# Reordering the first loads and two groups of matmuls in a linear-attention block on one core

## The chip, the core and the metric

The kernel runs on one NeuronCore of a Trainium2 chip. The core has a matrix engine (PE, with its weight loads listed as PEld), a vector engine (DVE), an activation engine (ACT, also called ScalarE), a general engine (POOL, also called GpSimd) and a queue engine (SP, also called SyncE). The engines run their own instruction streams in order and wait for each other by semaphores. DMAs are issued by SP and by ACT here, and 16 DMA engines of the core carry them. The metric is the device time in microseconds (us); the smaller, the better.

## The reference

One transformer block in bfloat16 with 2048 positions and width 640. With LN a layer norm without learned scale:

```python
h   = x + A(LN(x))            # linear attention, 32 heads of 20
out = h + B(LN(h))            # GEGLU: (gelu(h @ w_gate) * (h @ w_up)) @ w_down, inner width 1536

# A:
q, k, v = split(LN(x) @ wqkv)                 # each 2048 x 640, by heads
pq, pk  = q @ w_phi, k @ w_phi                # per head, 20 x 20
phi(y)  = [softmax(y), softmax(-y)]           # 40 features per head
kv, z   = phi(pk).T @ v, sum(phi(pk))         # over all positions
o       = (phi(pq) @ kv) / (phi(pq) . z + 1e-6)
A       = o @ wo
```

## The kernel before, in words

The 2048 positions are 16 tiles of 128, four to a block of 512. Tile t of `x` is `x_sb[t // 4][:, t % 4, :]`. The text calls tiles 0 to 3 x0 to x3.

The program is one hand-written order of instructions (L186 to L860) with no planner; each engine runs its instructions in the order in which they are written.

**Front (L186 to L491).** SP issues the loads of x0, x1, x2, two chunks of `Wv` (row blocks 0-1 and 2-3 of the v part of wqkv, 320 KB each), x3, the last `Wv` chunk (row block 4, 160 KB), tiles 4 and 5 of x, and then five transposing loads of the k part (`load_T`, L202). ACT issues only `wphi` (25 KB, 640 rows of 40 bytes) and then loads its function table (L191). PE warms up on constants. For tiles 0 and 1, x minus its mean (`xc`, L271 and L423) is transposed by PE and copied to `LN1T` by ACT (L164); the scale 1/std is applied later, when v is evicted (`v_ev`, L315). Tile 1's mean comes from an ACT pass (`st_act`, L406), tiles 0, 2, 3 and on from `BN_STATS` on DVE (L120). `v_part(t, *cs)` issues the matmuls of v of tile t for row blocks cs (two each, L311). `ln_tp(2)` is PE's transpose of tile 2 (L163) and DVE's copy of it (L164), which stands on DVE between the two statistics of tile 3. `root[0]()` is the pair Ln, Exp on ACT (L130, L131) that gives 1/std of tile 3. `fold` (L231) multiplies w_phi into the k part of wqkv, 128 rows at a time, by PE (L247), evicted by ACT (L256) or DVE (L258).

**The k loop (L493 to L533).** For each tile: k features by PE, exp(k) and exp(-k) on ACT (L339), their sums and reciprocals on DVE (L346, L350), the division by POOL and DVE (L354), v of a later tile (L295), and, for groups of tiles, the accumulation of phi(k).T @ v in one PSUM tile `kvp` (`kv_tile`, L373). Towards its end come the first q products, four groups.

**Turn (L534 to L542 and L782 to L833).** After the last `kv_tile`, DVE copies and masks `kvp` and transposes it into `KV[0]` and `KV[1]`, one for each sign of phi (L380, L382). `q_mm(j, part, kcs)` is the product of q of group j: two parts of five matmuls of 512 columns (L395), and `q_exp` its two exponentials on ACT (L400). `attn_a(t)` is phi(q) @ KV of tile t: 20 small products on `KV[0]`, then 20 on `KV[1]` (L587), and the copies of the result to `AB` by ACT and DVE (L606).

**The rest (L849 to L859)** weaves the gate/up matmuls (L721), the down matmuls (L740) and the remaining attention steps of each tile.

PSUM has four two-bank buffers in this half of the program, which all of `tp`, `pv`, `wa`, `pk`, `pq`, `ab` share (`gtile`, L110): a tile waits for the eviction of the one whose buffer it takes.

Of the kernel before, what the change touches and what calls it, by code (L numbers as in the profile page):

```python
# [17 lines left out]
def kernel(  # L18
# [12 lines left out]
    nc = tc.nc  # L31
    P = 128
    S = 2048
    D = 640
# [5 lines left out]
    NC = D // P  # L40
# [31 lines left out]
    x_v = A_x.rearrange("b (p t) d -> p (b t) d", t=NT)  # L72
    o_v = out.rearrange("b (p t) d -> p (b t) d", t=NT)
    w_v = A_wqkv.rearrange("(c p) n -> p c n", p=P)
# [9 lines left out]
    x_sb = [const.tile([P, 4, D], BF16, name=f"x_sb{b}") for b in range(NB)]  # L84
# [25 lines left out]
    def gtile(name):  # L110
        return psG.tile([P, 2, 512], F32, name=name, tag="G")

    def ln_stats(pool, tiles, tag, act=True, between=None, log=False):

        n = len(tiles)
        mv = small(pool, [P, n, nc.vector.BN_AGGR_DIM], "mv" + tag)
        stats = small(pool, [P, n, 2, nc.vector.BN_STATS_DIM], "stats" + tag)
        for j, xt in enumerate(tiles):
            for i in range(2):
                nc.vector.bn_stats(stats[:, j, i, :], xt[:, i * HD:(i + 1) * HD])  # L120
                if between and i == j == 0:
                    between()
        for j in range(n):
            nc.vector.bn_aggr(mv[:, j, :], stats[:, j])
        ve = small(pool, [P, n], "ve" + tag)
        rstd = small(pool, [P, n], "rstd" + tag)
        if log is not False:

            def root():
                nc.scalar.activation(ve, mv[:, :, 1], ACTF.Ln, bias=eps)  # L130
                nc.scalar.activation(rstd, ve, ACTF.Exp, scale=-0.5)  # L131

            if log is True:
                root()
            else:
                log.append(root)
        else:
            nc.gpsimd.tensor_scalar_add(ve, mv[:, :, 1], EPS)
            nc.gpsimd.tensor_tensor(rstd, ve, nhalf[:, 0:n], op=ALU.pow)

        mr = small(pool, [P, n], "mr" + tag)
        if act:
            for j in range(n):
                nc.gpsimd.tensor_scalar(mr[:, j:j + 1], mv[:, j, 0:1], rstd[:, j:j + 1], -1.0,
                                        op0=ALU.mult, op1=ALU.mult)
        return [(xt, mv[:, j, 0:1], rstd[:, j:j + 1], mr[:, j:j + 1]) for j, xt in enumerate(tiles)]
# [11 lines left out]
    def transpose_to(dst, src, on_pe, on_dve=False):  # L158

        if on_pe:  # L160
            tp = psG.tile([P, 16, P], BF16, name="tp", tag="G")
            for c in range(NC):
                nc.tensor.transpose(tp[:, c, :], src[:, c * P:(c + 1) * P], ident)  # L163
            (nc.vector.tensor_copy if on_dve else nc.scalar.copy)(dst, tp[:, 0:NC, :])  # L164
        else:
            nc.sync.dma_start_transpose(dst, src)
# [8 lines left out]
    Wv = p1.tile([P, NC, D], BF16, name="Wv")  # L175
# [9 lines left out]

    nc.gpsimd.memset(nhalf, -0.5)  # L186
    nc.gpsimd.memset(eps, EPS)
    nc.sync.dma_start(x_sb[0][:, 0:1, :], x_v[:, 0:1, :])
    nc.sync.dma_start(x_sb[0][:, 1:2, :], x_v[:, 1:2, :])
    nc.scalar.dma_start(wphi, phi_v.rearrange("(c p) f -> p c f", p=P))  # L190
    nc.scalar.add_instruction(mybir.InstLoadActFuncSet(name=nc.get_next_instruction_name(), act_func_set_id=6))  # L191
    nc.sync.dma_start(x_sb[0][:, 2:3, :], x_v[:, 2:3, :])
    nc.sync.dma_start(Wv[:, 0:2, :], w_v[:, 0:2, 2 * D:3 * D])
    nc.sync.dma_start(Wv[:, 2:4, :], w_v[:, 2:4, 2 * D:3 * D])
    nc.sync.dma_start(x_sb[0][:, 3:4, :], x_v[:, 3:4, :])
    nc.sync.dma_start(Wv[:, 4:5, :], w_v[:, 4:5, 2 * D:3 * D])
    nc.sync.dma_start(x_sb[1][:, 0:2, :], x_v[:, 4:6, :])

    def load_T(WT, i, *ds):
# [74 lines left out]
    def ln_st(*tiles, act=True, between=None, log=False):  # L274
        for t, v in zip(tiles, ln_stats(p1, [x_sb[t // 4][:, t % 4, :] for t in tiles], "1", act, between, log)):
            lnp[t] = v
# [8 lines left out]
    def ln_tp(t, on_dve=False):  # L285
        transpose_to(LN1T[t // 4][:, :, t % 4 * P:(t % 4 + 1) * P], lnp[t], True, on_dve)

    def lnT(t, c):
        b, tl = divmod(t, 4)
        return LN1T[b][:, c, tl * P:(tl + 1) * P]  # L290
# [14 lines left out]
    def v_part(t, *cs):  # L305

        if 0 in cs:
            pv[t] = gtile("pv")
        for c in cs:
            for u in range(2):  # L310
                nc.tensor.matmul(pv[t][:, u, 0:HD], lhsT=lnT(t, c), rhs=Wv[:, c, u * HD:(u + 1) * HD],  # L311
                                 start=(c == 0), stop=(c == NC - 1))

    def v_ev(t):
        nc.scalar.activation(vS[t % NV][:, :, 1:VC].rearrange("p (u h) f -> p u h f", u=2),  # L315
                             pv[t][:, :, 0:HD].rearrange("p u (h f) -> p u h f", f=Dh), ACTF.Copy,
                             scale=lnp[t][2] if t in CT else 1.0)
# [68 lines left out]
    def q_mm(j, part=(0, 1), kcs=range(NC)):  # L386

        if 0 in part and 0 in kcs:
            pqs[j] = gtile("pq")
        for i, bc in enumerate(QG[j]):  # L390
            if i not in part:
                continue
            b, c = divmod(bc, NC)
            for kc in kcs:
                nc.tensor.matmul(pqs[j][:, i, :], lhsT=Wq2[:, kc, c * P:(c + 1) * P], rhs=LN1T[b][:, kc, :],  # L395
                                 start=(kc == 0), stop=(kc == NC - 1))

    def q_exp(j, signs=(0, 1)):
        for s in signs:
            nc.scalar.activation(Eq[j][:, :, s, :], pqs[j][:, 0:len(QG[j])], ACTF.Exp, scale=(1.0, -1.0)[s])  # L400
# [49 lines left out]
    v_part(0, 2, 3)  # L450
    root = []
    ln_st(3, act=False, between=lambda: ln_tp(2, True), log=root)
    v_part(1, 2, 3)
    v_part(0, 4)
    root[0]()
    v_ev(0)
    v_part(1, 4)
    v_ev(1)
    v_part(2, *range(NC))
# [74 lines left out]
    q = len(QT)  # L534
# [67 lines left out]
    def attn_a(t, dve=0):  # L602
        attn_a_mm(t)
        AB, ab = ABs[t % 2], st[t, "ab"]
        for u in ((1, 0) if t in (4,) else (0, 1)):
            (nc.vector.tensor_copy if u >= 2 - dve else nc.scalar.copy)(  # L606
                AB[:, :, u * UH:(u + 1) * UH].rearrange("p s (r h) f -> p r s (h f)", r=2),
                ab[u][:, :, 0:2 * QH * KC].rearrange("p r (s x) -> p r s x", s=2))
        st[t] = AB
# [170 lines left out]


    q_mm(q, (0,))  # L782
    q_mm(q, (1,), (0, 1))
    attn_a(0, 1)
    q_mm(q, (1,), (2, 3, 4))
    q_exp(q)
    q_mm(q + 1)
    attn_b(0, True)
# [102 lines left out]
```

## Time and profile before

| what | us |
|---|---|
| median of 3 runs (272.98 to 273.24) | 272.99 |
| the profiled execution | 272.91 |
| its span, first to last instruction | 271.1 |
| PE busy in the span | 265.3 |
| DVE busy | 175.1 |
| ACT busy | 137.9 |
| POOL busy | 100.7 |
| granted clock of PE | 0.999 |

The profile lists instructions with their start from the beginning of the span, their length, the engine, the line of the kernel, and what they write and read (out<-in). A bracket at the end says how long the engine stood idle before the instruction and what ended the idle time. PE's matmuls are pipelined: they overlap, so the length of one is more than the distance to the next. A line that stands for several instructions says how many (x20).

### The profile page before, as it was taken

The page shows a single profiled execution, that of the slowest core. Times are in us where ns is not written, and L with a number is a line of the kernel's source. Part 1 is how long each engine was busy: PE and PEld are TensorE (multiplying, and loading weights), DVE is VectorE, ACT ScalarE, POOL GpSimd, SP SyncE. Part 2 cuts the span into 40 slices and gives each one's busy share as a digit, 9 for nine tenths or more (in the row PEclk, how much of TensorE's full clock was granted, in tenths as well). Part 3 has the DMA queues.
Part 4 walks back from the last instruction along what each step waited for, and adds up shares of the span by engine and source line. Part 5 has one row for each costly group of instructions (what it writes and reads, how often), then busy time and mean ns, then how long its engine had stood idle before and what let it go on. Part 6 is the DMA issues. An engine that isn't in the chain of part 4 may idle for free.

```text
span 271.1 us, 6984 instructions
## 1 busy us (share of the span) xinstructions
PE 265.3 (98%) x2843; PEld 170.7 (63%) x2862; DVE 175.1 (65%) x333; ACT 137.9 (51%) x238; POOL 100.7 (37%) x231
## 2 busy tenths in 40 slices
PE   7999999999999999999999999999999999999995
PEld 6777777764455887788755455774555576444574
DVE  5899999997877756694467783347768432333322
ACT  5769996887689675345524356114345600332100
POOL 5448889694002336384222564003165400000000
PEclk9999999999999999999999999999999999999999
DMA  7987357541787432232301222110122411000011
GB/s 189 221 201 171 53 98 89 57 104 52 232 271 223 150 99 59 69 73 51 73 4 51 48 48 51 48 52 0 51 48 48 52 48 51 24 0 0 2 48 48
DMA packets 45263, 22.10 MB, mean 81 GB/s; under 512 B 37808, under 2 KB 43184, under 8 KB 45232
## 3 DMA queue, kind: packets, MB, share of 16 engines
q1 hardware_dynamic: 44576, 21.64, 33.2%
q8 instruction: 22, 0.36, 0.5%
q10 hardware_dynamic: 656, 0.03, 0.2%
q14 instruction: 9, 0.07, 0.1%
HBM read 10.18 MB, written 2.62 MB: 47 GB/s over the span
## 4 chain that ended last, share of the span: by engine, by line
PE 85%; DVE 10%; DMA 2%; issue 1%; ACT 1%; SPq 0%; POOL 0%; DVEq 0%; POOLq 0%
PE gu L721 38%; PE pd L740 19%; PE po L661 8%; PE pq L395 7%; DVE sk L346 4%; PE pk L295 3%; DVE stats L120 3%; PE pv L295 3%; PE ab L587 2%; DMA Wv<-in_A_wqkv_dram 2%; PE kvp L373 1%; DVE rs L350 1%; PE wa L247 1%; DVE E L354 1%; PE pv L311 1%
## 5 line engine op out<-in xcount | busy, mean ns | idle before, releaser
L724 ACT ACTIVATE g<-gu 128x512 bf16<-128x512 f32 (+1 forms) x60 | 30.5, 510 | 63.4 <-PE gu L721 62.6
L727 DVE TENSOR_TENSOR GT<-gu,g 128x512 bf16<-128x512 f32 (+1 forms) x60 | 34.3, 578 | 43.9 <-PE gu L721 31.2
L721 PE MATMUL gu<-LN2T,Wg 128*128 128x512 bf16 (+1 forms) x287 | 61.2, 335 | 0.7
L721 PE MATMUL gu<-LN2T,Wu 128*128 128x512 bf16 (+1 forms) x300 | 61.8, 336 | 0.0
L740 PE MATMUL pd<-Wd,GT 128*128 128x320 bf16 (+2 forms) x396 | 53.5, 295 | 0.0
L740 PEld LDWEIGHTS <-GT 128*128 128x128 bf16 x396 | 37.9, 98 | 14.6 <-DVE GT L727 0.2
L721 PEld LDWEIGHTS <-Wu 128*128 128x128 bf16 x300 | 29.3, 98 | 22.6
L721 PEld LDWEIGHTS <-Wg 128*128 128x128 bf16 x300 | 28.6, 98 | 20.3
L295 PEld LDWEIGHTS <-LN1T 128*128 128x128 bf16 x290 | 27.9, 98 | 10.4
L743 DVE TENSOR_TENSOR y<-pd,x_sb 128x320 bf16<-128x320 f32 (+2 forms) x29 | 13.9, 479 | 29.5 <-PE pd L740 29.5
L354 POOL TENSOR_TENSOR E<-E,rs 128x640 bf16<-128x640 bf16 x24 | 30.2, 1288 | 6.5 <-DVE rs L350 2.6
L661 PE MATMUL po<-Wo,oT 128*128 128x320 bf16 x160 | 24.5, 299 | 0.0
L295 PE MATMUL pk<-Wk,LN1T 128*128 128x320 bf16 x160 | 24.4, 299 | 0.0
L395 PE MATMUL pq<-LN1T,Wq 128*128 128x512 bf16 x94 | 22.6, 379 | 0.3
L346 DVE TENSOR_REDUCE sk<-E 128x64 f32<-128x1280 bf16 x16 | 22.9, 1430 | 0.0
L400 ACT ACTIVATE Eq<-pq 128x1024 bf16<-128x1024 f32 (+1 forms) x26 | 19.9, 831 | 2.9 <-PE pq L395 2.7
L150 ACT ACTIVATE ln<-x_sb,v,rstd 128x640 bf16<-128x640 bf16 x14 | 12.9, 920 | 14.4 <-POOL v L700 14.3
L339 ACT ACTIVATE E<-pk 128x640 bf16<-128x640 f32 x28 | 18.7, 746 | 2.4 <-PE pk L295 1.8
L661 PEld LDWEIGHTS <-oT 128*128 128x128 bf16 x160 | 15.4, 98 | 6.9 <-ACT oT L164 0.2
L295 PE MATMUL pv<-Wv,LN1T 128*128 128x320 bf16 x130 | 19.8, 299 | 0.0
L636 DVE TENSOR_TENSOR tt<-AB,w 128x1280 bf16<-128x1280 f32 x12 | 17.8, 1486 | 1.0 <-POOL w L629 0.9
L616 POOL TENSOR_TENSOR pr<-AB 128x64 f32<-128x64 f32 x10 | 6.8, 677 | 26.7 <-DVE AB L597 20.6
(114 smaller groups left out, 289.6 us busy)
## 6 DMA issues: line engine op xcount, KB each, us to landing
out_dram<-y SPq DMA_DIRECT2D x15, 160.0 KB, 1.8
x_sb<-in_A_x_dram SPq DMA_DIRECT2D x6, 320.0 KB, 3.5
Wu<-in_B_w_up_dram SPq DMA_DIRECT2D x1, 1920.0 KB, 8.9
Wg<-in_B_w_gate_dram SPq DMA_DIRECT2D x2, 768.0 KB, 5.4
Wd<-in_B_w_down_dram SPq DMA_DIRECT2D x1, 1440.0 KB, 6.7
Wo<-in_A_wo_dram SPq DMA_DIRECT2D x1, 800.0 KB, 4.8
x_sb<-in_A_x_dram SPq DMA_DIRECT2D x4, 160.0 KB, 3.3
Wv<-in_A_wqkv_dram SPq DMA_DIRECT2D x2, 320.0 KB, 4.4
```

The source lines that it names most:

```text
L295: nc.tensor.matmul(ps[:, u, 0:HD], lhsT=lnT(t, c), rhs=W[:, c, u * HD:(u + 1) * HD], start=(c == 0), stop=(c == NC - 1))
L339: nc.scalar.activation(Ek[t][:, s, :].rearrange("p (u f) -> p u f", u=2), pk[:, :, 0:HD], ACTF.Exp, scale=((lnp[t][2], nrstd[t]) if t in C ...
L346: nc.vector.reduce_sum(sk, Ek[t].rearrange("p s (h f) -> p (s h) f", f=Dh), axis=AX.X)
L354: eng.tensor_tensor(e, e, rs[:, s * H:(s + 1) * H, None].to_broadcast([P, H, Dh]), ALU.mult)
L395: nc.tensor.matmul(pqs[j][:, i, :], lhsT=Wq2[:, kc, c * P:(c + 1) * P], rhs=LN1T[b][:, kc, :], start=(kc == 0), stop=(kc == NC - 1))
L400: nc.scalar.activation(Eq[j][:, :, s, :], pqs[j][:, 0:len(QG[j])], ACTF.Exp, scale=(1.0, -1.0)[s])
L636: nc.vector.tensor_tensor(tt.rearrange("p s (h f) -> p s h f", f=Dh), num, w[:, :, :, None].to_broadcast([P, 2, H, Dh]), ALU.mult)
L661: nc.tensor.matmul(pos[u], lhsT=st[t][:, c, :], rhs=Wo[:, c, u * HD:(u + 1) * HD], start=(c == 0), stop=(c == NC - 1))
L721: nc.tensor.matmul(gu[i][:, 0:n], lhsT=W[:, c, f * P:(f + 1) * P], rhs=LN2T[b][:, c, a0:a1], start=(c == 0), stop=(c == NC - 1))
L724: nc.scalar.activation(g[:, 0:n], gu[0][:, 0:n], ACTF.Gelu_apprx_tanh)
L727: nc.vector.tensor_tensor(st[b, "g", f][:, a0:a1], gu[1][:, 0:n], g[:, 0:n], ALU.mult)
L740: nc.tensor.matmul(ps, lhsT=st[b, "g", f][:, tl * P:(tl + 1) * P], rhs=Wd[:, f, f0:f1], start=(f == 0), stop=(f == NF - 1))
```

## The change

The three chunks of `Wv` are issued by ACT, right behind `wphi` and ahead of the table load. SP issues x0, x1, x2, x3, then tiles 4 and 5, then the transposing loads of the k part. The last row block of v of tile 0 and its eviction `v_ev(0)` are written ahead of the row blocks 2 and 3 of v of tile 1 and ahead of `root[0]()`. In the turn, the second part of the first late q group runs four of its five matmuls ahead of `attn_a(0, 1)` in place of two.

```diff
     nc.gpsimd.memset(nhalf, -0.5)
     nc.gpsimd.memset(eps, EPS)
-    nc.sync.dma_start(x_sb[0][:, 0:1, :], x_v[:, 0:1, :])
-    nc.sync.dma_start(x_sb[0][:, 1:2, :], x_v[:, 1:2, :])
     nc.scalar.dma_start(wphi, phi_v.rearrange("(c p) f -> p c f", p=P))
+    for c0, c1 in ((0, 2), (2, 4), (4, NC)):
+        nc.scalar.dma_start(Wv[:, c0:c1, :], w_v[:, c0:c1, 2 * D:3 * D])
     nc.scalar.add_instruction(mybir.InstLoadActFuncSet(name=nc.get_next_instruction_name(), act_func_set_id=6))
-    nc.sync.dma_start(x_sb[0][:, 2:3, :], x_v[:, 2:3, :])
-    nc.sync.dma_start(Wv[:, 0:2, :], w_v[:, 0:2, 2 * D:3 * D])
-    nc.sync.dma_start(Wv[:, 2:4, :], w_v[:, 2:4, 2 * D:3 * D])
-    nc.sync.dma_start(x_sb[0][:, 3:4, :], x_v[:, 3:4, :])
-    nc.sync.dma_start(Wv[:, 4:5, :], w_v[:, 4:5, 2 * D:3 * D])
+    for t in range(4):
+        nc.sync.dma_start(x_sb[0][:, t:t + 1, :], x_v[:, t:t + 1, :])
     nc.sync.dma_start(x_sb[1][:, 0:2, :], x_v[:, 4:6, :])
...
     v_part(0, 2, 3)
     root = []
     ln_st(3, act=False, between=lambda: ln_tp(2, True), log=root)
+    v_part(0, 4)
+    v_ev(0)
     v_part(1, 2, 3)
-    v_part(0, 4)
     root[0]()
-    v_ev(0)
     v_part(1, 4)
     v_ev(1)
     v_part(2, *range(NC))
...
     q_mm(q, (0,))
-    q_mm(q, (1,), (0, 1))
+    q_mm(q, (1,), (0, 1, 2, 3))
     attn_a(0, 1)
-    q_mm(q, (1,), (2, 3, 4))
+    q_mm(q, (1,), (4,))
     q_exp(q)
     q_mm(q + 1)
     attn_b(0, True)
```

## The prediction

> **What bounds the kernel now.** The page first: how busy each engine is, and the chain that ended last.
>
> ```profile
> PE 265.3 (98%) x2843; PEld 170.7 (63%) x2862; DVE 175.1 (65%) x333; ACT 137.9 (51%) x238; POOL 100.7 (37%) x231
> PE 85%; DVE 10%; DMA 2%; issue 1%; ACT 1%; SPq 0%; POOL 0%; DVEq 0%; POOLq 0%
> ```
>
> The kernel is a queue of matmuls, so I asked next for the engines' own time in three stretches, and for everything that PE waited for between 6 and 70 us.
>
> ```profile
> 12.40:40.40 28.00, 28.00 (x362) 20.35 (x360) 27.47 (x53) 25.83 (x40) 21.16 (x33) 1.00 0.64 132
> 70.00:271.00 201.00, 197.44 (x1807) 122.64 (x1821) 111.75 (x221) 82.21 (x151) 52.92 (x138) 1.00 0.25 66
> ```
>
> ```profile
> PE pv L311 <- DMA Wv<-in_A_wqkv_dram: 0.5, 1, 0.5
> PE ab L587 <- DVE KV L382: 0.3, 1, 0.3
> ```
>
> Columns of the stretches: length, then busy time of PE, PEld, DVE, ACT, POOL, the granted clock, DMA share, GB/s. From 12.4 to 40.4 us PE is full (28.00 of 28) and DVE nearly so (27.47). PE waits for W_v once and for KV once, and after 70 us for nothing. Which of the two full engines decides up to 40 us is told by the timeline there:
>
> ```profile
> 40.71 0.27 PEld L373 LDWEIGHTS <-vS 128*32 128x32 bf16 x32 [0.21 <-DVE E L354]
> ```
>
> PE stands 0.2 us until DVE has finished E. So a shift of DVE's chain before 40.7 us reaches the end one for one (a gain too, until PE itself is the later one), and a gain of PE alone reaches it only after that point. The timeline at the two edited places:
>
> ```profile
> 68.67 0.58 DVE L382 STREAM_TRANSPOSE KV<-KT 128x384 bf16<-128x384 bf16 x1
> 68.71 0.32 PE L587 MATMUL ab<-KV,Eq 32*128 32x44 bf16 x20
> 69.30 0.31 PE L587 MATMUL ab<-KV,Eq 32*128 32x44 bf16 x20 [0.27 <-DVE KV L382]
> 69.54 1.04 PE L395 MATMUL pq<-LN1T,Wq 128*128 128x512 bf16 x4
> ```
>
> ```profile
> 4.04 0.74 ACT L406 ACTIVATE sqa<-x_sb 128x640 bf16<-128x640 bf16 x1 [1.48 <-DMA x_sb<-in_A_x_dram]
> 5.62 0.89 DVE L120 BATCH_NORM_STATS2 stats<-x_sb 128x6 f32<-128x320 bf16 x2 [0.34 <-DMA x_sb<-in_A_x_dram]
> 6.49 1.79 PE L311 MATMUL pv<-Wv,LN1T 128*128 128x320 bf16 x12 [0.47 <-DMA Wv<-in_A_wqkv_dram]
> 8.12 0.44 PE L163 MATMUL tp<-ident,ln 128*128 128x128 bf16 x5
> 8.60 0.49 DVE L164 COPY LN1T<-tp 128x640 bf16<-128x640 bf16 x1 [0.22 <-PE tp L163]
> 9.77 0.29 ACT L130 ACTIVATE ve<-mv,eps 128x1 f32<-128x1 f32 x1 [1.64 <-DVE mv L124]
> ```
>
> And the loads in half-microsecond stretches:
>
> ```profile
> 3.00:3.50 0.50, 0.50 (x8) 0.50 (x6) 0.20 (x1) 0.00 (x0) 0.40 (x3) 1.00 0.97 283
> 3.50:4.00 0.50, 0.50 (x8) 0.50 (x6) 0.50 (x2) 0.00 (x0) 0.50 (x11) 1.00 1.01 120
> 4.00:4.50 0.50, 0.50 (x8) 0.50 (x6) 0.43 (x3) 0.46 (x1) 0.05 (x2) 1.00 0.69 115
> 5.00:6.00 1.00, 1.00 (x14) 0.70 (x14) 0.66 (x2) 0.85 (x4) 0.52 (x2) 1.00 0.95 326
> ```
>
> The DMA engines are full from 2.5 us on, but for one microsecond they move only 115 to 120 GB/s. x of tile 2, issued at 1.72, lands in that lull, at 5.6.
>
> **Part 1: two q products ahead of phi_q@KV.** No work is added. KV of the second sign ends at 69.25, and PE starts the second 20 products at 69.30, although the first 20 were issued from 68.71 on. The same 20 take 0.24 in the second group (69.30 to 69.54), so PE stands some 0.35 to 0.43. A q product costs 0.216 (the chain has 20 in 4.48 from 73.30, the last one's 0.16 overhang off), two cost 0.43. With them ahead the first group starts at 69.14 and the second at 69.3 to 69.38. Gain: 0.43 if the whole group of 20 issues in the 0.16 left, 0.36 if it takes 0.24. I take 0.43, as the first group's last weight load is issued within 0.23 of 68.71. Behind it on PE is q+1, with no wait. Late next would be ACT, which frees the buffer that q+2 needs: its second exponential runs 71.32 to 72.34, and q+2 would start at 72.86 - 0.43 = 72.43. That fits by 0.09; if ACT slips more than that, so does the gain. DVE's copy of AB (69.78) stays. From 70 us on PE waits for nothing, and what the others do there starts from PE's products, so the 0.43 reaches the end.
>
> **Part 2: v of tile 0 first.** Two products (0.27) pass four others on PE, nothing is added. v_ev(0) leaves 10.20 for about 8.9 to 9.7, into ACT's idle 1.64 before 9.77. If that cover is missed, the root behind it (9.77, which DVE's ln at 10.33 waits for) moves by what v_ev sticks out: start to start 0.68 (10.20 to 10.88), from 8.95 that is 9.63: fits by 0.14. v_ev(1) moves from 10.88 to 10.20, which frees the second fold's buffer; PE stood 0.27 there (11.44 to 11.71). But the next product of PE, v of tile 3 at 12.39, waits for the cast of the first fold (11.64 to 12.33), and that follows the first fold, not v_ev. Late next is that cast: gain 0, at most 0.05.
>
> **Part 3: the loads.** ACT gets three DMA issues. At SP's spacing for the same ones (2.18, 2.66, 3.18; 3.69, 4.16) they take 0.48 + 0.52 + 0.47 = 1.47. The table load, 1.28 at 1.28, moves to 2.75 and ends at 4.03; what follows waits for x of tile 1 until 4.04. Hidden with 0.01 to spare. A slip delays xc of tile 1 (4.90 to 5.28) and DVE's next, which now waits for x2 until 5.62: cover 0.34. SP loses three issues (1.42): x3 leaves at 2.18 (3.18 before), x(4,5) between 2.66 and 4.16, the W_k transposes and all that follow up to 1.5 earlier. None of those is waited for in this trace, so 0 for them, unless they take room from W_v (below).
>
> W_v chunk 0-1 is issued at 1.28 in place of 2.18. PE's first v product can start when LN1T of tile 0 is copied, 6.15 (its weight load is issued there), so at best 0.34 earlier. But the transposes of tile 2 (8.12) wait for ln of tile 2 too, 7.54 + 0.44 = 7.98, and DVE's copy of them at 8.60 starts the chain that sets everything up to 40.7. So W_v alone is worth 8.12 - 8.03 = 0.09. More comes only if x of tile 2 lands earlier: then DVE starts at 5.30 in place of 5.62, ln follows 0.32 sooner, and PE, with 12 products of 0.136 from 6.15, is free at 7.78: best case 0.34. If x2 lands late, its lateness counts in full, less the same 0.09.
>
> How x2 lands is what this trace can't show, since ACT's queue carries 25 KB only (w_phi, 2.8 us to landing beside x0). Bounds: it stays first and misses the lull (at 283 to 326 GB/s the microsecond at 117 lost some 170 KB, 0.5 us): 5.1. It comes behind the 320 KB of W_v: those take 0.8 to 1.0 at 326 to 395 GB/s, so 6.5. I take 5.7, near the row it has now and a little late, as 320 KB more compete for engines that are full. Its 0.1 of lateness is what the 0.09 covers: the front is worth 0.
>
> [...]
>
> **Sum.** 0.43 + 0 + 0 = 0.43 off. The profiled execution took 272.91 for a span of 271.1, 1.8 outside it; it stands 0.08 below the median 272.99. So a span of 270.7, 272.5 for such an execution, 272.6 as a median.
>
> **Rivals.**
> A. The front gains too: x2 lands before 5.6 and W_v before 6.3. For it: the lull is one microsecond of one trace, and issue is no longer in line. Against: no byte is saved. Front 0.12 to 0.34, time 272.2 to 272.45.
> B. x2 falls behind W_v, since two queues now take turns on the engines and W_v's chunk is at the head of the second one. Price: lands at up to 6.5, chain 0.9 - 0.09 = 0.81 later, less 0.43: 273.4; x1 (xc at 4.90 now, with 0.34 to spare) pushed back the same way would add up to 0.5. It decides from a landing after 6.1; before that the q products still win. For it: while w_phi ran, from 2.5 to 3 us, the rate was 243 GB/s with a share of 1.35, so the engines do serve both queues at once. Against: w_phi's short rows say little of 1280 B rows. [...]
> C. W_v chunk 2-3 falls behind x3 and x(4,5), now ahead on their own queue. It lands at 7.3 and is used at 7.58. 480 KB more in front are 1.2 to 1.5: up to 8.8, the transposes at 9.4, 1.25 late, less 0.43: 273.8. It decides from 8.0. Against: it is issued 0.9 earlier than now.
> D. The gain of part 1 is swallowed because ACT's exponentials free the buffers late (70 to 78 us has 7.35 of 8 busy): front 0.05, time 273.0.
>
> **How the numbers follow.** A measurement of this kernel tells about 0.2% (0.55 us) from no change, so faster is below 272.44, slower above 273.54. Forecast (272.45 to 272.95): 0.44. A: 0.30. B: 0.14, of it 0.08 past 273.54, with x1 late too. C: 0.08, 0.06 of it past that. D: 0.04. That gives 0.30 faster, 0.56 same, 0.14 slower. The range leaves out the last tenth on each side: 272.1 (A's best, 0.43 + 0.34 off, and 0.1 for the spread of three runs, 272.98 to 273.24) to 273.6, between B's end and C's. The likeliest case's own range is 272.45 to 272.95.
>
> **What will show it.** Part 1: no wait of PE for KV near 69 us; ab ends by 69.6 and q+1 starts at 69.77 relative to this trace. Part 2: v_ev(0) before the root, PE's pause in the folds gone, v of tile 3 no earlier. Part 3: the table load ending near 4.0, the DVE statistics of tile 2 at 5.3 to 5.8, the copy of its transposes at 8.5 to 8.7. I am wrong if x2's statistics start after 6.1, if PE waits for W_v before the transposes, or if a new wait on ACT stands between 70 and 78 us.

## The result, and the profile after

The changed kernel takes 274.61 us (median of 22 runs, 273.63 to 275.35) against 273.08 for the kernel before (22 runs beside them, 272.69 to 274.84). The ratio is 1.0047, interval 1.0038 to 1.0056, so it is slower, by 1.5 us in the medians and 1.3 by the ratio, where 272.6 was forecast. The profiled execution took 274.76 for a span of 273.0 (before: 272.91 and 271.1). The page of the changed kernel, its engines and its chain:

```profile
PE 266.9 (98%) x2862; PEld 170.7 (63%) x2862; DVE 175.1 (64%) x333; ACT 137.9 (51%) x238; POOL 101.0 (37%) x231
...
PE 85%; DVE 9%; DMA 4%; issue 1%; POOL 0%; DVEq 0%; POOLq 0%
```

The chain now holds 4% of DMA where it held 2%; the span has 1.9 us more and PE is busy 1.6 longer in it (the profile counts pipelined overlap as busy). The full stretch in the middle has only moved. From 14.7 to 42.7 us, that is 2.3 us later than in the kernel before (columns as there: PE, PEld, DVE, ACT, POOL, granted clock, DMA share, GB/s):

```profile
14.70:42.70 28.00, 27.99 (x358) 20.35 (x358) 27.28 (x53) 25.85 (x40) 21.19 (x33) 1.00 0.55 119
```

PE 27.99 of 28 and DVE 27.28, as before. So the loss lies ahead of it. PE's waits from 6 to 70 us in the changed kernel:

```profile
PE tp L163 <- DVE xc L420: 1.0, 1, 1.0
PE pv L308 <- DMA Wv<-in_A_wqkv_dram: 1.0, 1, 1.0
PE tp L163 <- DVE ln L155: 0.2, 1, 0.2
```

The wait for KV is gone from this list (part 1 of the change). The wait for xc of tile 1 is new, and the wait for W_v is 1.0 for its last chunk, where it was 0.5 for the first. The timeline of the changed kernel's front (start, length, engine, line, what is written and read, idle time and its releaser):

```profile
1.28 2.64 ACTq L190 DMA_DIRECT2D Wv<-in_A_wqkv_dram  x3
...
3.95 1.28 ACT L191 ACT_TABLE_LOAD   x1 [3.95 <-DMA wphi<-in_A_w_phi_dram]
...
6.10 0.39 DVE L420 TENSOR_SCALAR xc<-x_sb,va 128x640 bf16<-128x640 bf16 x1 [1.24 <-ACT sqa L403]
...
6.89 0.89 DVE L120 BATCH_NORM_STATS2 stats<-x_sb 128x6 f32<-128x320 bf16 x2 [0.40 <-DMA x_sb<-in_A_x_dram]
...
9.30 0.45 PE L163 MATMUL tp<-ident,ln 128*128 128x128 bf16 x5 [0.20 <-DVE ln L155]
...
10.73 2.60 PE L308 MATMUL pv<-Wv,LN1T 128*128 128x320 bf16 x18 [0.98 <-DMA Wv<-in_A_wqkv_dram]
...
11.20 0.79 ACT L312 ACTIVATE vS<-pv,rstdc 128x640 bf16<-128x640 f32 x1 [1.80 <-PE pv L308]
...
11.89 0.28 ACT L130 ACTIVATE ve<-mv,eps 128x1 f32<-128x1 f32 x1
...
12.45 0.45 DVE L155 TENSOR_SCALAR ln<-x_sb,mv,rstd 128x640 bf16<-128x640 bf16 x1 [1.16 <-ACT rstd L131]
```

Read it in four steps, each beside its time before.

1. ACT's three W_v issues take 2.64, not 1.47: the third starts at 3.55 only. The table load behind it starts at 3.95 (before 1.28), released by the landing of w_phi, which it does not read. In the trace's records the first eight loads count up eight completion semaphores in turn (numbers 100 and 103 to 109); the third W_v issue is the ninth load in that order, gets w_phi's semaphore (100) a second time, carries a wait for it, and starts 0.02 after w_phi's landing (3.53).
2. x of tile 2 lands at 6.87 (before 5.60). Fourteen of the 16 DMA engines had brought their share by 5.55; the last one was 1.3 later. It is not a lack of rate: from 4 to 6 us the loads move 350 GB/s, where the kernel before moved 264. DVE's statistics of tile 2 start at 6.89 (5.62).
3. W_v's last chunk lands at 10.69 (8.12). PE reaches the product that needs it right behind the transposes of tile 2, and waits until 10.73.
4. The eviction of v of tile 0 waits for that product, and the root of tile 3 (`ve`, 11.89, before 9.77) stands behind it on ACT, though its input was there by 10.9. DVE's ln of tile 3 starts at 12.45 (10.33): 2.12 late, and with the folds 2.31 at the place where PE waits for DVE's E (43.02 against 40.71):

```profile
43.02 0.27 PEld L370 LDWEIGHTS <-vS 128*32 128x32 bf16 x32 [0.20 <-DVE E L351]
```

The gain sits at the turn. The changed kernel there:

```profile
69.36 2.12 PE L392 MATMUL pq<-LN1T,Wq 128*128 128x512 bf16 x9
...
71.41 0.47 PE L584 MATMUL ab<-KV,Eq 32*128 32x44 bf16 x40
71.81 1.47 PE L392 MATMUL pq<-LN1T,Wq 128*128 128x512 bf16 x6
```

All 40 products run in one group without a wait, and q+1 follows at once. 2.31 late less 0.43 gives the 1.9 by which the span grew.

So three causes are candidates for the front: the late table load, x of tile 2 late, and W_v's last chunk late with the root behind it. They overlap in time, so the trace alone can't say what each costs.

### The profile page after: what moved, and what is told of

Same layout as the page of the kernel before. It is cut to its first block, busy times and chain, and to the rows that moved or that the text cites. A ratio compares the mean times of both kernels' runs of the same rounds, so it can differ in the third digit from the quotient of the medians.

```text
span 273.0 us, 7003 instructions
## 1 busy us (share of the span) xinstructions
PE 266.9 (98%) x2862; PEld 170.7 (63%) x2862; DVE 175.1 (64%) x333; ACT 137.9 (51%) x238; POOL 101.0 (37%) x231
## 4 chain that ended last, share of the span: by engine, by line
PE 85%; DVE 9%; DMA 4%; issue 1%; POOL 0%; DVEq 0%; POOLq 0%
PE gu L718 38%; PE pd L737 19%; PE pq L392 8%; PE po L658 8%; DVE sk L343 3%; PE pk L292 3%; DMA Wv<-in_A_wqkv_dram 3%; PE pv L292 3%; DVE stats L120 2%; PE ab L584 2%; PE kvp L370 1%; DVE rs L347 1%; PE wa L244 1%; DMA wphi<-in_A_w_phi_dram 1%; PE pv L308 1%
```

## The experiments

Differences are medians against the kernel before in the same set of runs; the interval is that of the ratio, 0.001 being 0.27 us. The ratio is not the quotient of the medians; the two differ by up to 0.25 us. A trace is one execution; where it lies far from the median of its kernel and that matters, the text says so.

### Each part alone

```diff
 # e_q: the kernel before, and only
-    q_mm(q, (1,), (0, 1))
+    q_mm(q, (1,), (0, 1, 2, 3))
     attn_a(0, 1)
-    q_mm(q, (1,), (2, 3, 4))
+    q_mm(q, (1,), (4,))
```

> Only the q products are moved (part 1), all else as before. First theory (this part does what was forecast, and the loss lies elsewhere): PE's wait for KV of 0.43 us near 69 us is gone, the time falls by 0.43, to 272.65 beside 273.08. Rival (ScalarE's queue behind it takes the gain): no change, 273.1, with a new wait for ScalarE behind 70 us.

Measured: 272.61 against 273.08, ratio 0.9985 (0.9976 to 0.9993). Its timeline:

```profile
67.21 2.12 PE L395 MATMUL pq<-LN1T,Wq 128*128 128x512 bf16 x8
69.26 0.47 PE L587 MATMUL ab<-KV,Eq 32*128 32x44 bf16 x40
69.66 2.55 PE L395 MATMUL pq<-LN1T,Wq 128*128 128x512 bf16 x10
```

0.47 gained, and the hole of the kernel before (69.03 to 69.30) is not there. Part 1 does what was forecast.

```diff
 # e_v: the kernel before, and only
+    v_part(0, 4)
+    v_ev(0)
     v_part(1, 2, 3)
-    v_part(0, 4)
     root[0]()
-    v_ev(0)
```

> Only the order of v of tile 0 is changed (part 2), loads and q as before. First theory (harmless when the last chunk of W_v has landed in time, 8.12 in the trace before): 272.9 to 273.3, the eviction of v of tile 0 ends before the variance of tile 3 is there. Rival (the order alone delays the root of tile 3): the root moves by 0.3 to 0.7 and the end with it, 273.4 to 273.8.

Measured: 273.18 against 273.08, ratio 1.0006 (0.9996 to 1.0015): nothing that can be told. In its trace v of tile 0 is evicted from 8.76 and the root starts at 9.66. With W_v in time, the order is harmless, as forecast.

```diff
 # e_loads: the changed kernel, order of v and of the q products as before
-    v_part(0, 4)
-    v_ev(0)
     v_part(1, 2, 3)
+    v_part(0, 4)
     root[0]()
+    v_ev(0)
...
-    q_mm(q, (1,), (0, 1, 2, 3))
+    q_mm(q, (1,), (0, 1))
     attn_a(0, 1)
-    q_mm(q, (1,), (4,))
+    q_mm(q, (1,), (2, 3, 4))
```

> Only the loads are changed (part 3), the order of v and q as before. First theory (the third W_v issue on ScalarE waits for w_phi to land, because its completion semaphore is used a second time, and the table load stands behind it): the table load begins at 3.9 instead of 1.28, the sum for tile 1 at 5.2 instead of 4.04, everything behind moves by 1.1 to 1.3, so 274.2 to 274.4. Rival one (the new order of v of tile 0 is the whole loss, the front has slack): 273.1. Rival two (the two queues compete for the DMA engines): the same 1 us and more, but then VectorE waits longest for x of tile 2, over 1 us, and not for ScalarE.

Measured: 274.88 against 273.08, ratio 1.0062 (1.0043 to 1.0080). So the loads carry the loss, 1.8 of it here, and more than expected. The granted clock tells why this one execution lost more (stretches of 2 us, columns as above):

```profile
6.00:8.00 2.00, 1.44 (x12) 1.15 (x13) 1.85 (x5) 1.94 (x7) 0.52 (x2) 0.72 1.28 267
8.00:10.00 2.00, 2.00 (x9) 1.14 (x8) 1.17 (x3) 1.00 (x3) 0.76 (x2) 0.50 0.94 152
10.00:12.00 2.00, 2.00 (x18) 1.48 (x17) 1.11 (x4) 0.00 (x0) 1.57 (x7) 0.93 1.14 213
```

PE paused from 5.1 to 6.56 for the late xc of tile 1 and ran at half its clock from 6.87 to 10.28: 9 matmuls in 2 us, where the kernel before has 20. That happened in three of the six runs (mean clock 0.993 or 0.994, times 275.19 to 275.80) and in two of the 22 of the changed kernel (0.994), which are not its slowest (274.72, 274.85). It is a cost that the late table load can bring, not the one that the changed kernel mostly pays.

The three parts alone add up to -0.47 + 0.10 + 1.80 = 1.43; together they are 1.53. That they nearly agree is partly luck: the three runs of e_loads at the full clock have a median of 274.35, by which the sum is 0.90, and the order of v, harmless alone, costs some 0.4 in company (e_oldv below).

### Which of the loads' three effects

```diff
 # e_two: the changed kernel, W_v in two issues
-    for c0, c1 in ((0, 2), (2, 4), (4, NC)):
+    for c0, c1 in ((0, 2), (2, NC)):
```

> The whole change, but W_v comes in two issues (chunks 0 and 1, then 2 to 4) instead of three, so that no issue on ScalarE is the ninth DMA. First theory (the reused semaphore is the cause): ScalarE issues its DMAs without a wait, the table load ends by 3.7, the sum for tile 1 starts when x of tile 1 lands near 4.0; the front loses 0.3 at most, and the time is 272.6 to 272.9. Rival (the two queues compete for the DMA engines): x of tile 2 lands near 6.9 and W_v's last chunks after 8.4 as in the changed kernel, and 0.8 us or more stays in the front: 273.5 or more.

Measured: 273.46 against 273.08, ratio 1.0014 (0.9998 to 1.0031), twelve runs from 272.59 to 275.26. Its timeline:

```profile
1.28 1.06 ACTq L190 DMA_DIRECT2D Wv<-in_A_wqkv_dram  x2
2.38 1.28 ACT L191 ACT_TABLE_LOAD   x1 [2.38 <-issue]
...
7.29 0.89 DVE L120 BATCH_NORM_STATS2 stats<-x_sb 128x6 f32<-128x320 bf16 x2 [2.01 <-DMA x_sb<-in_A_x_dram]
...
8.85 0.70 PE L308 MATMUL pv<-Wv,LN1T 128*128 128x320 bf16 x4 [0.51 <-DMA Wv<-in_A_wqkv_dram]
...
11.93 0.45 DVE L155 TENSOR_SCALAR ln<-x_sb,mv,rstd 128x640 bf16<-128x640 bf16 x1 [0.24 <-ACT rstd L131]
```

With eight loads no issue of ScalarE waits (the two of W_v take 1.06), and 1.15 of the loss is back (274.61 to 273.46). The other 0.85 against the q products alone (272.61) stays: DVE now waits 2.0 for x of tile 2. (The profiled execution took 274.18, 0.7 above the median, so its landing, 7.27, is on the late side.) Both readings were half right. But two things went with the ninth load, the late table load and the late last chunk (8.81 here). The next run parts them.

```diff
 # e_tab: the changed kernel, the table load ahead of the three W_v issues
+    nc.scalar.add_instruction(mybir.InstLoadActFuncSet(...))
     for c0, c1 in ((0, 2), (2, 4), (4, NC)):
         nc.scalar.dma_start(Wv[:, c0:c1, :], w_v[:, c0:c1, 2 * D:3 * D])
-    nc.scalar.add_instruction(mybir.InstLoadActFuncSet(...))
```

> The changed kernel with the table load ahead of the three W_v issues. The run with two issues showed that a DMA issue does not wait for a table load ahead of it, so W_v's first two issues stay at 1.3 and 1.85; the third now waits for x of tile 1 (near 4.0), which the sum for tile 1 behind it needs anyway, so that sum begins at 4.1 to 4.4 instead of 5.24, and the last chunk still lands after 10. First theory (the late table load carries the 1.15): 273.4 to 273.7. Rival (the late last chunk of W_v, with the root of tile 3 behind the eviction that needs it): 274.3 to 274.6.

Measured: 274.47 against 273.25, ratio 1.0049 (1.0031 to 1.0067): the changed kernel's own loss. Its timeline:

```profile
1.28 1.28 ACT L189 ACT_TABLE_LOAD   x1 [1.28 <-PEq L872]
1.31 3.13 ACTq L191 DMA_DIRECT2D Wv<-in_A_wqkv_dram  x3
...
6.84 0.89 DVE L120 BATCH_NORM_STATS2 stats<-x_sb 128x6 f32<-128x320 bf16 x2 [1.10 <-DMA x_sb<-in_A_x_dram]
...
10.73 2.60 PE L308 MATMUL pv<-Wv,LN1T 128*128 128x320 bf16 x18 [1.03 <-DMA Wv<-in_A_wqkv_dram]
...
12.44 0.45 DVE L155 TENSOR_SCALAR ln<-x_sb,mv,rstd 128x640 bf16<-128x640 bf16 x1 [1.21 <-ACT rstd L131]
```

The table is there at 2.56, xc of tile 1 at 5.35 instead of 6.10, and nothing is won: DVE waits for x of tile 2 anyway (6.84 against 6.89), and ln of tile 3 starts at 12.44 against 12.45. So my first theory, that the late table load carries the loss, falls. In the changed kernel it is hidden behind x of tile 2. What the wait costs comes through W_v's last chunk, whose issue waits here for x of tile 1 (4.07) and lands at 10.68 (10.69 there). The profiled execution is the slowest of its six (275.56): its span is 0.8 longer than the changed kernel's, and PE waits 0.70 at 89 us for a transposing load (LN2T), far behind the front.

```diff
 # e_oldv: the changed kernel, order of v of tile 0 as before
-    v_part(0, 4)
-    v_ev(0)
     v_part(1, 2, 3)
+    v_part(0, 4)
     root[0]()
+    v_ev(0)
```

> The changed kernel with the order of v of tile 0 as before (loads and q products stay). First theory (the loads carry the loss, the order nearly nothing, as the runs with one part alone add up): 274.88 less 0.47, 274.4, within 0.3 of the changed kernel's 274.61. Rival (in the changed kernel the root of tile 3 stands behind v of tile 0, which waits for W_v's last chunk, and that costs what its trace reads, 1.1): 273.5.

Measured: 274.18 against 273.08, ratio 1.0040 (1.0025 to 1.0055). The chunk lands as late (10.35), but four products now stand ahead of PE's wait and the root ahead of the eviction: ln of tile 3 starts at 11.17. 0.43 better than the changed kernel, with intervals that overlap, and not far above the 0.3 that e_tab3 below shows for equal kernels: between both expectations. The order, harmless alone, puts the root behind the late chunk; but PE stops for the chunk in either order, so only part comes back.

```diff
 # e_sp4: the changed kernel, W_v's last chunk on SyncE behind x3
-    for c0, c1 in ((0, 2), (2, 4), (4, NC)):
+    for c0, c1 in ((0, 2), (2, 4)):
...
     for t in range(4):
         nc.sync.dma_start(x_sb[0][:, t:t + 1, :], ...)
+    nc.sync.dma_start(Wv[:, 4:5, :], w_v[:, 4:5, 2 * D:3 * D])
```

> The changed kernel with W_v's last chunk issued by SyncE behind x of tile 3, as before the change, the other two by ScalarE. First theory (no issue on ScalarE waits, so the 1.15 us of the reused semaphore is gone; the transposes start 0.5 us later than with two issues, so less of the rest stays): 272.7 to 273.3. Rival (any W_v on ScalarE's queue delays x of tile 2): 273.4 or more.

Measured: 273.57 against 273.08, ratio 1.0013 (0.9999 to 1.0027), from 272.50 to 274.29. The chunk lands at 7.81, the wait on ScalarE is gone, and so is a good 1 us, as with two issues. What stays is again x of tile 2 (6.22, in an execution of 273.04, 0.5 below the median).

### What a late x of tile 2, a late ScalarE and the transposes cost

```diff
 # e_x2late: the kernel before, x2 behind W_v's first chunks on SyncE
-    nc.sync.dma_start(x_sb[0][:, 2:3, :], ...)
     nc.sync.dma_start(Wv[:, 0:2, :], ...)
+    nc.sync.dma_start(x_sb[0][:, 2:3, :], ...)
```

> The kernel before with x of tile 2 issued by SyncE behind the first two chunks of W_v instead of ahead of them; ScalarE's queue is untouched. First theory (whatever lets W_v pass x of tile 2 costs what x is late, one queue or two): x of tile 2 lands near 6.4 instead of 5.6, W_v's first chunks near 5.6 instead of 6.45, the end moves by 0.8: 273.9. Rival (the earlier W_v makes up for it): 273.1 to 273.3.

Measured: 273.79 against 273.25, ratio 1.0024 (1.0014 to 1.0033).

```profile
6.12 0.89 DVE L120 BATCH_NORM_STATS2 stats<-x_sb 128x6 f32<-128x320 bf16 x2 [0.81 <-DMA x_sb<-in_A_x_dram]
6.13 1.85 PE L311 MATMUL pv<-Wv,LN1T 128*128 128x320 bf16 x12
```

The statistics start 0.50 later (6.12 against 5.62), DVE's copy of tile 2's transposes 0.42 later (9.02 against 8.60), and this execution, the fastest of its ten (273.28), has a span 0.35 longer; the medians differ by 0.54. So a late x of tile 2 counts nearly one for one, though W_v came sooner (5.68 against 6.45). It was late by less than expected (6.09, not 6.4), so the sum was smaller.

```diff
 # e_late: the kernel before, ScalarE kept busy on constants before st_act
+    for n in (512, 512, 512, 512, 128):
+        nc.scalar.activation(sqa[:, 0:n], ones[:, 0:n], ACTF.Identity)
     st_act(1, 0)
```

> The kernel before with five extra ScalarE instructions on constants (their output is overwritten) between the table load and the sum for tile 1, so that ScalarE is free for it at about 5.2, as late as with the late table load of the changed kernel (5.24); no DMA is touched. First theory (the late table load reaches the end): VectorE's statistics of tile 2 move from 5.62 to 6.4, the end by 0.8: 273.9. Rival (slack behind it): 273.1 to 273.4.

Measured: 275.15 against 273.25, ratio 1.0062 (1.0044 to 1.0080). Its timeline:

```profile
6.41 0.39 DVE L423 TENSOR_SCALAR xc<-x_sb,va 128x640 bf16<-128x640 bf16 x1 [1.57 <-ACT sqa L406]
...
7.78 2.75 PE L311 MATMUL pv<-Wv,LN1T 128*128 128x320 bf16 x12
...
10.85 0.49 DVE L164 COPY LN1T<-tp 128x640 bf16<-128x640 bf16 x1 [1.25 <-PE tp L163]
```

The delay came out longer than meant (the sum for tile 1 at 5.54, 1.5 late, not 1.2), and PE, after a pause of 1.5 in its weight loads, took 2.75 for the twelve products of v that took 1.79 before: most of them start 0.27 apart, where the kernel before has 0.136. (This trace holds no record of the granted clock.) So a late ScalarE is dear where x of tile 2 is in time, here 1.9, of which some 1.0 is PE at half its rate; in the changed kernel it was covered. This run prices the danger, not the changed kernel's loss.

```diff
 # e_hold: two issues, and W_k's transposing loads held until W_v is there
-    for c0, c1 in ((0, 2), (2, 4), (4, NC)):
+    for c0, c1 in ((0, 2), (2, NC)):
...
-    load_T(WkT, 1, *range(NC))
...
     ln_st(2, act=False, log=True)
+    nc.gpsimd.tensor_copy(WkT[:, 0, 0:1], Wv[:, NC - 1, 0:1])
+    load_T(WkT, 1, *range(NC))
```

> The changed kernel with W_v in two issues, and the five transposing loads of W_k held back until W_v has landed (a one-element copy on GpSimd from W_v into W_k's tile). First theory (what is left in the front with two issues, 273.46 against 272.61, is the transposing loads starting while W_v's packets are still moving: packets stood still until 9.5 there): no packet of a plain load takes over 1 us, W_v has landed by 7.3, the time is 272.6 to 272.9. Rival (the two queues compete from 3 to 6 us, before any transposing packet): x of tile 2 still lands 0.5 us late and more, and 273.2 to 273.6 stays. If the held transposes come too late for the folds, TensorE waits for WkT at a fold near 11 to 18 us.

Measured: 278.33 against 273.08, ratio 1.0195 (1.0181 to 1.0208). Its timeline:

```profile
6.88 0.89 DVE L120 BATCH_NORM_STATS2 stats<-x_sb 128x6 f32<-128x320 bf16 x2 [1.58 <-DMA x_sb<-in_A_x_dram]
8.96 0.70 PE L307 MATMUL pv<-Wv,LN1T 128*128 128x320 bf16 x4 [1.23 <-DMA Wv<-in_A_wqkv_dram]
...
16.97 0.78 PE L243 MATMUL wa<-BD,WkT 128*128 128x140 bf16 x6 [2.85 <-DMA WkT<-in_A_wqkv_dram]
```

As a time it is useless, since the folds starve (3.5 of waits for WkT). As a test it decides one thing: the first transposing packet moves at 10.7, no packet of a plain load takes over 1 us, and still x of tile 2 lands at 6.86 and W_v's end at 8.92. So the transposes are not what makes these late. What is left is W_v on the second queue: where SyncE alone issued W_v's first chunks ahead of x of tile 2 (e_x2late), x of tile 2 landed at 6.09 and W_v's end at 8.02.

### Trying to keep x of tile 2 in time

```diff
 # e_tabtwo: two issues, and the table load ahead of them
+    nc.scalar.add_instruction(mybir.InstLoadActFuncSet(...))
     for c0, c1 in ((0, 2), (2, NC)):
         nc.scalar.dma_start(Wv[:, c0:c1, :], ...)
-    nc.scalar.add_instruction(mybir.InstLoadActFuncSet(...))
```

> The changed kernel with W_v in two issues and the table load ahead of them, so W_v's packets start 1.3 us later than in the run with two issues alone (273.46). First theory (what remains there is W_v's packets passing x of tile 2 on the shared DMA engines): x of tile 2 lands by 5.8, the front loses 0.2 at most, 272.6 to 272.9. Rival (ScalarE's W_v costs whatever its start): 273.3 or more.

Measured: 273.48 against 273.25, ratio 1.0010 (0.9996 to 1.0024). The delay I counted on did not come: W_v was issued at 1.32, beside the table load (1.29). e_two's trace had shown only the reverse order, a table load that started behind the issues ahead of it (2.38). x of tile 2 lands at 6.68: in effect the kernel of e_two, and its time. The theory was not tested by this run.

```diff
 # e_x2act: two issues, and x2 ahead of W_v on ScalarE's queue
     nc.scalar.dma_start(wphi, ...)
+    nc.scalar.dma_start(x_sb[0][:, 2:3, :], x_v[:, 2:3, :])
     for c0, c1 in ((0, 2), (2, NC)):
         nc.scalar.dma_start(Wv[:, c0:c1, :], ...)
...
-    for t in range(4):
+    for t in (0, 1, 3):
```

> The changed kernel with W_v in two issues and x of tile 2 issued by ScalarE ahead of them instead of by SyncE. First theory (W_v's packets pass x of tile 2 on the shared DMA engines, and its last packets come 0.6 to 1.7 late): x of tile 2 lands by 5.2, VectorE's statistics of tile 2 begin by 5.4, and the time is 272.2 to 272.7 with a narrower spread. Rival (W_v itself, or the transposing loads, are what is late): 273.3 or more.

Measured: 276.06 against 273.25, ratio 1.0101 (1.0087 to 1.0115). Its timeline:

```profile
5.32 0.88 DVE L120 BATCH_NORM_STATS2 stats<-x_sb 128x6 f32<-128x320 bf16 x2
...
8.66 2.43 PE L309 MATMUL pv<-Wv,LN1T 128*128 128x320 bf16 x12 [2.16 <-DMA Wv<-in_A_wqkv_dram]
...
11.66 0.49 DVE L164 COPY LN1T<-tp 128x640 bf16<-128x640 bf16 x1 [3.40 <-PE tp L163]
```

x of tile 2 is in at 4.98 as hoped, and W_v's first chunks now last until 8.62 (14 of 16 engines by 7.43). PE pauses 2.2, its mean granted clock is 0.994 in all five runs (1.000 or 0.999 in the kernel before), and the time is the worst of this group. In both orders tried with W_v on the second queue something is late; the order chose what.

```diff
 # e_best: the kernel before with the q products, and x2 on ScalarE alone
     nc.scalar.dma_start(wphi, ...)
+    nc.scalar.dma_start(x_sb[0][:, 2:3, :], x_v[:, 2:3, :])
...
-    nc.sync.dma_start(x_sb[0][:, 2:3, :], x_v[:, 2:3, :])
```

> The kernel before with the q products moved (272.61 alone) and x of tile 2 issued by ScalarE behind w_phi; W_v stays on SyncE. First theory (what VectorE waits for in the front is x of tile 2): it lands near 5.0 instead of 5.6, W_v 0.4 sooner, and the time is 272.1 to 272.4. Rival (the front is bound by x of tile 1 and ScalarE): 272.6.

Measured: 272.93 against 273.25, ratio 0.9988 (0.9979 to 0.9997). x of tile 2 lands at 4.47 and its statistics start at 5.27, 0.35 sooner, but W_v's first chunks land at 6.45 as before, PE starts v at 6.50, and DVE's copy of tile 2's transposes stays at 8.60. So the first theory misses: the ratio is that of the q products alone (0.9985). The front of the kernel before has two paths of nearly one length, x of tile 2 and W_v, and shortening the first alone gains nothing; shortening W_v alone was not tried.

```diff
 # e_wphi: the kernel before with the q products, w_phi behind the table load
-    nc.scalar.dma_start(wphi, ...)
     nc.scalar.add_instruction(mybir.InstLoadActFuncSet(...))
+    nc.scalar.dma_start(wphi, ...)
```

> The kernel before with the q products moved (272.61 alone) and w_phi's load issued behind the table load instead of ahead of it, so that its 640 small packets come after those of x of tiles 0 and 1. First theory (loads on two queues share the DMA engines, so what is not urgent should start later): x of tiles 0 to 2 land 0.2 to 0.4 sooner and the time is 272.2 to 272.4. Rival (small packets cost nothing, or the mask product at 6.7 waits for w_phi): 272.6 or more.

Measured: 272.60 against 273.25, ratio 0.9979 (0.9970 to 0.9988). The issue again did not wait for the table load (0.82, beside 0.79), so the loads of x did not move: it is a second measurement of the q products alone, 272.60 beside 272.61.

```diff
 # e_tab3: the kernel before, the table load written three times
+    nc.scalar.add_instruction(mybir.InstLoadActFuncSet(...))
+    nc.scalar.add_instruction(mybir.InstLoadActFuncSet(...))
```

> The kernel before with the function table loaded three times in a row in place of once (the second and third change nothing): by rows of 1.28 us the last load ends at 5.12, as late as the single one of the changed kernel (5.23), and no DMA is touched. First theory (a late table load reaches the end one for one): the sum for tile 1 begins at 5.12 instead of 4.04 and the time grows by 1.08, to 274.15. Rival (there is slack behind it, the loss came from the DMAs): 273.1 to 273.5.

Measured: 273.39 against 273.08, ratio 1.0013 (1.0004 to 1.0021). Its trace holds one table load, at 1.28; the two repeats are not in it. So it prices nothing, but it shows how far a kernel with the same instructions in the front can come out from the kernel before: 0.3 us. Differences of that size are not read here.

## Why the prediction was wrong

**Bound: right.** A shift of DVE's chain ahead of 40.7 us reaches the end one for one: 2.31 at that place, less 0.43, is the span's 1.9. e_x2late shows nearly the same: 0.42 at DVE's copy of tile 2, 0.35 in the span.

**Part 1: right.** Forecast 0.36 to 0.43, measured 0.47 (0.19 to 0.66) in e_q. Rival D (ScalarE swallows it) did not come: the profiled execution of the changed kernel has no wait of PE from 60 to 75 us.

**Part 2: right alone, wrong in company.** Forecast 0, measured 0.10 with an interval across zero. The sentence "if that cover is missed, the root behind it moves by what v_ev sticks out" named the mechanism; the step failed in taking W_v's last chunk as landed. In the changed kernel v_ev(0) ran at 11.20, not 8.9, and pushed the root by about 1.

**Part 3: here it failed, at two steps.** All three marks set for it were missed: the table load ended at 5.23 (4.0 forecast), the statistics of tile 2 started at 6.89 (5.3 to 5.8), the copy of its transposes at 9.79 (8.5 to 8.7).

The first is "ACT gets three DMA issues ... they take 1.47 ... hidden with 0.01 to spare". The issues themselves took 0.54, 0.49 and 0.36. What I missed is the wait of the third, the ninth load of the program, for the landing of the first. The trace before shows that wait on SP: x(4,5), its ninth load, carries it and is issued at 4.16, after w_phi's landing at 3.61, where nobody was hurt. I took its issue time as spacing and did not ask which instruction takes that place after the move; no rival held this wait. The cost was 1.15 (274.61 against 273.46 with two issues; 0.9 by the ratios), and it came not by the table load, for which I had kept an eye open, but by W_v's last chunk: issued at 3.55 instead of about 2.4 (where the second issue ends), landing at 10.35 to 10.69 in the four traces with three issues, 8.25 to 8.92 in the three that have two issues in the same place of the queue, 7.81 in e_sp4, where SyncE issued it.

The second is the landing of x of tile 2, "I take 5.7", between bounds of 5.1 and 6.5. This was rival B, with a chance of 0.14 and a price of 273.4 for a landing of up to 6.5. With two issues, the premise of part 3 fulfilled, the median was 273.46; the landing was 7.27 in the profiled execution of e_two (274.18) and 6.68 in that of e_tabtwo (273.56). Rival B's own sum (the lateness, less 0.09, less 0.43) fits both: it gives 1.15 and 0.56, and the spans grew by 1.26 and 0.64. Its other half did not come: x of tile 1 landed at 3.96 to 4.07 in all eight kernels of that kind (4.01 before). Over the traces: with all of W_v on SyncE, and x of tile 2 ahead of it, the last engine delivered x of tile 2 between 5.08 and 5.80 (six kernels); with two or three chunks on ScalarE and x of tile 2 on SyncE between 6.06 and 7.27 (eight kernels). The bound of 6.5 assumed that all engines serve W_v first. The traces have it otherwise: most engines bring x of tile 2 by 5.2 to 6.2, and the last one or two are late (in the changed kernel fifteen by 5.56, the last at 6.87). The premise that the engines are full from 2.5 us on was also too strong: the prediction's own row from 4.0 to 4.5 us has a share of 0.69, and the changed kernel filled that lull (0.96 and 333 GB/s there, 115 before) without x of tile 2 coming sooner.

The prediction's sum put part 3 at 0. The runs agree that there is no gain, and with two issues they put it at 0.85 below nothing (273.46 against 272.61), as x of tile 2 lands later beside W_v (7.27 in e_two, 5.60 before).

Rival C (W_v chunk 2-3 behind x3 and x(4,5)) was seen in part: that chunk landed at 8.36 in place of 7.28, but PE stood behind ln of tile 2 by then, so it decided nothing. Rival A, the front gains, is excluded for the median; the best runs of e_two and e_sp4 (272.59, 272.50) come down to the best ones of the q products alone (272.37) and no lower.

The version to keep is the q products alone: 272.61 and 272.60 in two sets of runs. No version here beats it.

Open: why one or two DMA engines fell behind in these traces when two queues were fed, and so why e_two, e_tabtwo and e_sp4 spread from 272.5 to 275.3 where e_q spreads from 272.4 to 273.2. The traces tell only when each engine finished.

## What to carry to other kernels

When a load is moved to another engine's queue, write down for every load which completion semaphore it will use: here eight served in turn, the ninth load waited on its issuing engine for the first to land (until 3.55), and what stood behind it on that engine (the table load, 3.95 in place of 1.28) and its own data (10.69 in place of 8.12) were late with it. Do not count on rate from a second queue where the DMA engines are busy already: here the changed kernel moved 296 GB/s from 2 to 8 us, the kernel before 288, and the last of 16 engines decided when a load was there (x of tile 2 at 6.87, fifteen of them done by 5.56). And if a step is put ahead of a short one that others wait for (an eviction ahead of a root), ask what happens when its data is a microsecond late, not only whether it fits when all is in time.

## What the runs showed of the hardware

- **A DMA issue on ScalarE did not wait for a table load ahead of it, but a table load started only behind the DMA issues ahead of it.** 1.31 beside 1.28 in e_tab, 0.82 beside 0.79 in e_wphi; 2.38 behind two issues in e_two, 3.95 behind a waiting one in the changed kernel.
- **With W_v on a second queue, the last engine trailed more.** With W_v on SyncE, the last engine brought x of tile 2 from 0.04 to 0.54 after the fourteenth (0.17 in the kernel before); with W_v on ScalarE from 0.3 to 1.46 (1.32 in the changed kernel), and in e_x2act W_v's first chunks trailed by 1.19.
- **Where transposing loads started while plain ones moved, some packets stood still for a while.** In e_two 19 packets of 256 bytes took 0.64 to 2.06 us and all ended near 9.52, when SyncE's issue of the third transposing load ended (2.48 us long, the median of the five 1.51). In the changed kernel 17 packets, 13 of W_v and 4 of 256 bytes, took 0.76 to 1.59 us and ended from 8.59 to 8.68; its third transposing issue (1.77 long) ended at 8.63. What stopped them is not shown. e_hold shows that this was not what made x of tile 2 late (6.86 there, with no packet of a plain load over 1 us).
- **In some executions PE ran at half its clock; in e_loads this came behind pauses in its work.** There its weight loads paused for 0.76 and 1.43 us, and the granted clock was 0.50 from 6.87 to 10.28. In the 3.41 us before that (3.46 to 6.87) PE was busy for 1.57; in the changed kernel, whose longest pause was 1.2, it was busy for 2.25 of the 3.42 from 8.69 to 12.11, and the clock stayed at 1.00. The mean clock was 0.994 in every run of e_x2act (a pause of 2.16) and of e_hold (pauses of up to 3.03), 0.993 or 0.994 in three of the six of e_loads, 0.994 in two of the 22 of the changed kernel. Why the same kernel lost its clock in some executions only was not tested.
